# Eight early chunks in place of four in the output stage of a fused attention and spectral-mixing kernel

## The chip, the core and the metric

The kernel runs on one core of a Trainium2 chip. The metric is the device time of one execution in microseconds. The profile is of one execution; the timed runs are others. The engines are named as in the profile: PE is TensorE (PEld its weight loads), DVE is VectorE, ACT is ScalarE, POOL is GpSimd, SP is SyncE, which here only issues DMAs.

## What is computed

The first half is attention with a feature map, for 8 batches, 8 heads, 576 tokens and 64 features a head; the second half takes its output as x (8 batches, 576 tokens, 512 channels), mixes the 64 lowest frequencies of each sequence, and adds a rectified product.

```python
def _moe_ref(x, w_r, w_i, w_ch):
    X = np.fft.rfft(x, axis=1)
    Y = np.zeros_like(X)
    Xr, Xi = (np.real(X[:, :n_modes]), np.imag(X[:, :n_modes]))
    Yr = np.einsum('bmd,mde->bme', Xr, w_r) - np.einsum('bmd,mde->bme', Xi, w_i)
    Yi = np.einsum('bmd,mde->bme', Xr, w_i) + np.einsum('bmd,mde->bme', Xi, w_r)
    Y[:, :n_modes] = Yr + 1j * Yi
    y = np.fft.irfft(Y, n=S, axis=1)
    u = x + y
    return u + np.maximum(u @ w_ch, 0.0)
```

The weights w_r and w_i are 64 x 512 x 512 each in float32; most of what the kernel reads is these. The output is 8 x 576 x 512 float32, 9.44 MB.

## The kernel before

The core holds x in SBUF as `xs`, cut into 36 chunks `(bp, n)`: bp is one of four pairs of batches, n from 0 to 8; chunks 0 to 3 belong to the first batch of the pair, 4 to 7 to the second, and chunk 8 has rows of both. Every chunk has 128 tokens and 512 channels. A chunk's output is p + relu(q), where p = x + y and q = (x + y) w_ch. The kernel works with linearity: `xw` holds x w_ch of each chunk, and the contribution of the frequencies is added to both by matmuls with an inverse-transform table, from `yall` (the mixed frequencies) into p, and from `zall` (these times w_ch) into q.

The 64 frequencies are worked on in eight octets, `o` = 0 to 7. The weights of an octet come by GpSimd's DMA queue, in the order `wq`, into buffers of the pool `pw` (eight of them, tag "wt", which later also hold `yall`, `yl` and the output tiles). `mix` multiplies them; at the end of an octet its result is staged in `yst`, multiplied by w_ch into `zst`, and `put` copies both by DMA to their places: octets 0 to 6 to `yall` and `zall`, octets 6 and 7 also to `yl`, four copies at four groups of 32 partitions.

While the weights of the last groups arrive, `fill` takes pieces of other work from the list `todo`. A piece is the transposing of a chunk and its product with w_ch (`Channels`, 36 pieces, which also step through `inverse_tables`, where VectorE makes the tables CI, CD, CL and CM), or the adding of the octets that are already there (`Absorb`): octets 0 to 5 (96 rows of `yall` and `zall`) for most chunks, octets 0 to 6 (112 rows) for the early ones, which `full` puts last.

After the last octet stands the output stage, written out by hand as a list `seq` of `Last` objects: two single chunks, pairs of chunks, and two single chunks at the end. Each is one of these kinds:

- early: its last octet is added with table CM straight from `yst` and `zst` (`straight`), in full matmuls with 128 rows. These are chunks (0,0) to (0,3) before. The tiles hold eight batches' rows, so the table has zeros for all batches but the chunk's own.
- normal: octets 6 and 7 are added from `yl` with table CL (`late`), in matmuls with 32 rows that sit at different partitions for p and q and for the two chunks of the pair. x is brought into p by a matmul with the permutation `perm` (`base(0)`), xw into q by another (`base(1)`).
- later, "GpSimd pairs" below: chunks in `stored`, and the ninth chunks. Their x was written back to SBUF in the permuted order while filling (`back_x`), p gets no x on TensorE, and GpSimd adds x to the rectified q in SBUF (`relu`).

For all, ACT rectifies q out of PSUM into `rl` or `rx`, VectorE adds p and this into the output tile `of` (`ofr` for single chunks), and SP issues the store. Chunk (0,0) differs: ACT copies p into `rl` ahead of time (`keep_p`), and VectorE does max(q, 0) + rl in one instruction. q has four PSUM banks in turn (`bank`), p two double banks (`banks`), `rl` two buffers. All engines keep the program's order; `ahead` says which pair's q is worked on in front of which pair's p.

Of the kernel before, what the change touches and what calls it, by code (L numbers as in the profile page):

```python
# [43 lines left out]
def kernel(  # L44
# [536 lines left out]
    stored = [(1, 0), (1, 1), (1, 4), (1, 5), (2, 0), (2, 1), (2, 6), (2, 7), (3, 4), (3, 5)]  # L581
# [3 lines left out]
    CM = CF.rearrange("p c t x m -> p (c t x m)")[:, 0:512].rearrange("p (c s) -> p c s", c=4)  # L585


    def inverse_tables():
# [33 lines left out]
        jm, tm, rm, b0 = bits(pi, 5, 3), bits(pi, 4, 1), bits(pi, 3, 1), bits(pi, 0, 7)  # L622
        last = calc(calc(tm, 4.0, jm), 1.0, 56.0)
        b0 = calc(b0, 0.0, 1.0, ALU.is_equal, ALU.mult)
        yield
        for dst, m, r, only in ((CI, mode, r, None), (CL, late, r, None), (CM, last, rm, b0)):
            n = 512 if only is not None else 640
            ph = calc(r, -S_ / 4.0, S_ / 4.0)
            amp = calc(r, -4.0 / S_, 2.0 / S_)
            if m is mode:  # L630
                half = calc(calc(m, 0.0, -0.5, ALU.is_equal, ALU.mult), 1.0, 1.0)
                amp = calc(amp, half, 0.0)
            if only is not None:
                amp = calc(amp, only, 0.0)
            dve.tensor_scalar(out=ang[:, :n], in0=tok[:, :n], scalar1=m, scalar2=ph,
                              op0=ALU.mult, op1=ALU.add)
            dve.tensor_scalar(out=rnd[:, :n], in0=ang[:, :n], scalar1=1.0 / S_, scalar2=MAGIC,
                              op0=ALU.mult, op1=ALU.add)
            dve.tensor_scalar(out=rnd[:, :n], in0=rnd[:, :n], scalar1=-MAGIC,
                              scalar2=-float(S_), op0=ALU.add, op1=ALU.mult)  # L640
            dve.tensor_tensor(out=ang[:, :n], in0=ang[:, :n], in1=rnd[:, :n], op=ALU.add)
            yield
            act.activation(rnd[:, :n], ang[:, :n], ACT.Sin, scale=2.0 * math.pi / S_)
            if dst is CI:
                dve.tensor_scalar_mul(out=dst.rearrange("p c s -> p (c s)"), in0=rnd[:, :n],
                                      scalar1=amp)
                yield
                for a in range(2):
                    dve.tensor_copy(
                        CD.rearrange("k c (p a) -> k a c p", a=2)[:, a],  # L650
                        CI[:, 0:4].rearrange("k c (a p) -> k a c p", a=2)[:, a])
                yield
                continue
            for c in range(4):
                dve.tensor_scalar_mul(
                    out=dst[:, c, :].rearrange("k (p a) -> k a p", a=2),
                    in0=rnd[:, 128 * c:128 * c + 128].rearrange("k (a p) -> k a p", a=2),
                    scalar1=amp)
            if dst is CL:
                dve.tensor_scalar_mul(out=dst[:, 4, :], in0=rnd[:, 512:640], scalar1=amp)  # L660
            yield
# [46 lines left out]
    class Absorb:  # L708

        def __init__(self, bp, n):  # L710
            self.bp, self.n = bp, n
            self.table = CD if (bp, n) in stored else CI
            self.early = bp == 0 and n < 4
            self.rows = slice(0, 112 if self.early else 96)
# [71 lines left out]
    def put(src, o, dst, copies):  # L786
        if o < 7:
            sp.dma_start(dst[16 * o:16 * o + 16], src)
        if o > 5:
            for s in copies:  # L790
                r = 32 * s + 16 * (o - 6)
                (pool if o == 6 else act if s == 3 else sp).dma_start(yl[r:r + 16], src)


    class Last:

        def __init__(self, *items):
            self.items = items
            bp, n = items[0]
            self.early = bp == 0 and n < 4  # L800
# [32 lines left out]
        def straight(self, which):  # L833
            if self.early:
                for a, (bp, n) in enumerate(self.items):
                    pe.matmul((self.q if which else self.p)[a], lhsT=CM[:, n],
# [18 lines left out]
        def store(self):  # L855
# [5 lines left out]
            if n == 0 and self.first:  # L861
# [18 lines left out]
    seq = [Last((0, 0)), Last((0, 1))] + [Last(*x) for x in pairs[0][1:] + pairs[1] + pairs[2]]  # L880
    seq += [Last(*x) for x in pairs[3][:3]] + [Last((3, 6)), Last((3, 7))]
    seq.insert(11, Last((0, 8), (1, 8)))
    seq.insert(15, Last((2, 8), (3, 8)))
    H = DMODEL // 2
    while mixq:
# [4 lines left out]
        if not mixq:  # L890
            assert not todo
            seq[0].base(1)
            seq[0].late(1)
            seq[0].base(0)
            seq[0].late(0)
# [4 lines left out]
        if g == NG - 1 and i == 1:  # L900
            end = left == 0
            if end:
                seq[1].base(1)
                seq[1].late(1)
# [37 lines left out]
        else:  # L942
            fill(n)
    assert not todo
    seq[1].late(0)
    seq[2].base(1)
    seq[0].straight(1)
    seq[1].straight(0)
    seq[1].straight(1)
    seq[1].relu()  # L950
    ahead = {1: [2], 2: [3], 3: [4, 5], 4: [7], 5: [6], 6: [9], 7: [8], 8: [11], 9: [10], 10: [13],
             11: [12], 12: [15], 13: [14], 14: [17], 15: [16], 16: [18], 17: [19], 18: []}
    for g, s in enumerate(seq):
        ts = [seq[i] for i in ahead.get(g, [])]
        if ts and g not in (1, 3):
            ts[0].base(1)
        if g > 1 and g != 3:
            s.base(0)
        if g == 2:
            s.straight(0)  # L960
            seq[4].base(1)
            seq[3].base(0)
        for t in ts[:1]:
            t.late(1)
        if g > 2:
            s.late(0)
        for t in ts[:1]:
            t.straight(1)
            t.relu()
        s.store()  # L970
        for t in ts[1:]:
            t.base(1)
            t.late(1)
            t.relu()
# [31 lines left out]
```

## Time and profile before

| | |
|---|---|
| time, median of 4 runs (lowest to highest) | 443.27 us (442.14 to 444.83) |
| the profiled execution: time; span from first to last instruction | 441.98 us; 440.1 us |
| mean granted TensorE clock over the span | 0.909 |
| busy: PE, DVE, ACT, POOL | 334.7, 287.4, 282.7, 101.3 us |
| DMA read from and written to HBM | 163.64 MB, 9.44 MB |
| last weight lands | 403.52 us from the span's start |
| first and last store issued | 408.40 and 434.45 us |

A row of the table of stretches gives, for each stretch of time, its length, then the busy time of each engine with the number of its instructions, the granted clock, the mean busy share of the 16 DMA engines, and GB/s. The share can exceed 1 where packets overlap. A row of the timeline gives start, duration, engine, line, operation, the tile written and those read, with shapes; in square brackets stands how long the engine was idle before, and what it waited for. All rows carry line L37, the helper that issues every instruction, so tiles tell them apart: `pp` is p, `pt` is q, `of` the output of a pair.

### The profile page before, as it was taken

Reading aid. Unit: us, or ns where it says so; the run is one execution under the profiler, and the core shown is the slowest. Engines: PE = TensorE matmul, PEld = TensorE weight load, DVE = VectorE, ACT = ScalarE, POOL = GpSimd, SP = SyncE. Lnnn points to the kernel's source line nnn. Section 1 sums busy time; section 2 is a strip of 40 time slices with the busy share of each in tenths; the row PEclk is TensorE's granted clock in tenths of the full one; section 3 lists DMA queues with packets and bytes.
Section 4 is the critical chain, followed back from the end, with each engine's and each line's share of the span. In section 5 each row is a group of like instructions: output and inputs, shape, how many; then the busy total and the mean of one; then the engine's idle time right before and its main releaser. Section 6 shows DMA issues by size and latency. Waiting matters only on the chain.

```text
span 440.1 us, 10584 instructions
## 1 busy us (share of the span) xinstructions
PE 334.7 (76%) x4451; PEld 213.5 (49%) x4451; DVE 287.4 (65%) x563; ACT 282.7 (64%) x498; POOL 101.3 (23%) x142
## 2 busy tenths in 40 slices
PE   3567668777696677786886786947689999999992
PEld 2346547545565555664664564633345544433220
DVE  4667586555666766876777668638863343876694
ACT  4598687666878875985886768513544442665781
POOL 7132132121312212322322111131001120010391
PEclk9689888688989988997997899797999999999997
DMA  8999999999999999999999999999999999996697
GB/s 173 236 210 210 238 212 237 235 214 264 210 213 236 238 236 228 221 237 211 239 212 237 225 224 239 212 212 212 212 218 219 219 224 221 212 219 138 211 390 294
DMA packets 51584, 99.58 MB, mean 226 GB/s; under 512 B 2512, under 2 KB 13648, under 8 KB 51536
## 3 DMA queue, kind: packets, MB, share of 16 engines
q0 software_dynamic: 45376, 86.45, 99.7%
q1 hardware_dynamic: 6016, 12.32, 7.9%
q8 instruction: 35, 0.57, 0.5%
q10 hardware_dynamic: 144, 0.13, 0.2%
q14 instruction: 13, 0.11, 0.1%
HBM read 163.64 MB, written 9.44 MB: 393 GB/s over the span
## 4 chain that ended last, share of the span: by engine, by line
DMA 42%; issue 23%; PE 16%; DVE 7%; POOL 6%; ACT 4%; POOLq 0%; DVEq 0%; ACTq 0%
DMA wt<-in_moe_w_i_dram 29%; PE pt L37 12%; DMA vn<-in_v_dram 6%; DMA wt<-in_moe_w_r_dram 5%; POOL wt L37 3%; PE two L37 2%; PE one L37 1%; ACT AB L37 1%; ACT xw L37 1%; DVE xw L37 1%; POOL qb L37 1%; DMA out_dram<-of 1%; PE pp L37 1%; POOL kb L37 1%; DMA yl<-zst 1%
## 5 line engine op out<-in xcount | busy, mean ns | idle before, releaser
L37 ACT ACTIVATE AB<-two 128x1024 bf16<-128x1024 f32 x64 | 62.2, 1032 | 11.9 <-DVE mk L37 9.4
L37 ACT ACTIVATE AQ<-two 128x1024 bf16<-128x1024 f32 x64 | 62.9, 1051 | 3.6 <-PE two L37 3.4
L37 ACT CAST xw<-pt 128x512 bf16<-128x512 f32 x50 | 29.4, 587 | 40.7 <-PE pt L37 40.7
L37 DVE TENSOR_REDUCE mk<-two 128x8 f32<-128x1024 f32 x32 | 38.9, 1218 | 15.3 <-PE two L37 15.3
L37 DVE TENSOR_REDUCE m<-two 128x8 f32<-128x1024 f32 x32 | 39.2, 1224 | 12.9 <-PE two L37 12.7
L37 DVE RECIPROCAL rd<-one 128x6 f32<-128x6 f32 x48 | 9.4, 196 | 50.4 <-PE one L37 50.3
L37 DVE TENSOR_TENSOR va<-vn,ee 128x1152 bf16<-128x1152 f32 x32 | 42.0, 1355 | 0.0
L37 PE MATMUL pt<-wchb,xT 128*128 128x512 bf16 x136 | 35.8, 386 | 7.0 <-DVE xT L37 5.7
L37 POOL DMA_DIRECT2D wt<-in_moe_w_r_dram x30 | 22.3, 744 | 71.6 <-PE one L37 31.1
L37 POOL DMA_DIRECT2D wt<-in_moe_w_i_dram x28 | 20.9, 747 | 74.7 <-PE one L37 42.6
L37 PEld LDWEIGHTS <-xs 128*128 128x128 bf16 x624 | 31.6, 103 | 12.6 <-issue 7.7
L37 ACT COPY kT<-one 128x512 bf16<-128x512 bf16 (+1 forms) x32 | 19.2, 640 | 28.6 <-PE one L37 28.4
L37 PEld LDWEIGHTS <-minus 96*128 96x128 bf16 x288 | 27.7, 115 | 18.5 <-issue 13.4
L37 PE MATMUL two<-w2blk,qT 128*128 128x256 bf16 x128 | 20.3, 283 | 20.9 <-ACT AB L37 11.1
L37 PE MATMUL one<-wt,XT 128*32 128x512 bf16 x304 | 27.8, 452 | 9.8 <-DMA wt<-in_moe_w_i_dram 4.3
L37 PE MATMUL two<-qT,w2blk 128*128 128x512 bf16 x64 | 29.9, 467 | 4.4 <-ACT AQ L37 4.2
L37 PEld LDWEIGHTS <-qT 128*128 128x128 bf16 x144 | 13.8, 98 | 37.3 <-issue 35.1
L37 PE MATMUL two<-mT,minus 96*128 96x128 bf16 x256 | 30.3, 252 | 0.0
L37 POOL DMA_DIRECT2D kb<-in_k_dram x16 | 11.5, 718 | 75.5 <-PE one L37 74.7
L37 PE MATMUL one<-kvz,AQ 128*128 128x65 bf16 x512 | 28.0, 211 | 0.0
L37 DVE TENSOR_TENSOR xs<-one,rd 128x384 bf16<-128x384 f32 x48 | 26.8, 557 | 1.6
L37 PEld LDWEIGHTS <-XT 128*32 128x32 bf16 x512 | 14.4, 149 | 25.6 <-issue 12.3
(141 smaller groups left out, 725.8 us busy)
## 6 DMA issues: line engine op xcount, KB each, us to landing
wt<-in_moe_w_r_dram POOLq DMA_DIRECT2D x30, 1024.0 KB, 24.9
wt<-in_moe_w_i_dram POOLq DMA_DIRECT2D x28, 1024.0 KB, 24.7
vn<-in_v_dram POOLq DMA_DIRECT2D x15, 576.0 KB, 19.5
out_dram<-of SPq DMA_DIRECT2D x16, 512.0 KB, 3.4
kb<-in_k_dram POOLq DMA_DIRECT2D x16, 288.0 KB, 17.4
qb<-in_q_dram POOLq DMA_DIRECT2D x16, 288.0 KB, 17.2
xs<-in_moe_w_i_dram POOLq DMA_DIRECT2D x2, 1024.0 KB, 24.7
yacc<-in_moe_w_r_dram POOLq DMA_DIRECT2D x1, 1024.0 KB, 9.1
```

Of the source, the lines that this page charges most:

```text
L37: ins = f(*args, **kwargs)
```

## The change

The early chunks become (0,0) to (0,7). For the second batch of the first pair of batches a second table CM is made, whose zeros are elsewhere; CL and each CM are now written by one VectorE instruction over four chunks instead of four. The chunks (1,0), (1,1), (1,4), (1,5), (3,4) and (3,5) leave `stored`, (2,4) and (2,5) join it, so that there are three GpSimd pairs in place of five, besides the two pairs of ninth chunks. Chunk (0,1) is handled as (0,0) was. The last copy of `zst` into `yl`, which ACT's queue issued, is issued by SP. The order of the output stage is written anew: the pairs (1,0) to (1,6) are normal and follow each other, and the q of pair (2,0) is worked on behind pair (1,0).

```diff
--- before.py
+++ after.py
@@ -578,11 +578,12 @@
     CI = pb.tile([128, 5, 128], BF16, name="CI", bufs=1)
     CL = pb.tile([128, 5, 128], BF16, name="CL", bufs=1)
     CD = pb.tile([128, 4, 128], BF16, name="CD", bufs=1)
-    stored = [(1, 0), (1, 1), (1, 4), (1, 5), (2, 0), (2, 1), (2, 6), (2, 7), (3, 4), (3, 5)]
+    stored = [(2, 0), (2, 1), (2, 4), (2, 5), (2, 6), (2, 7)]
     perm = CF.rearrange("p c t x m -> p (c t x m)")[:, 512:640]
     dve.tensor_copy(perm.rearrange("k (p a) -> k a p", a=2),
                     ident_b.rearrange("k (a p) -> k a p", a=2))
-    CM = CF.rearrange("p c t x m -> p (c t x m)")[:, 0:512].rearrange("p (c s) -> p c s", c=4)
+    CM = [CF.rearrange("p c t x m -> p (c t x m)")[:, 0:512].rearrange("p (c s) -> p c s", c=4),
+          pb.tile([128, 4, 128], BF16, name="CM", bufs=1)]
 
 
     def inverse_tables():
@@ -619,19 +620,17 @@
         jt = calc(t, 4.0, j)
         mode = calc(bits(pi, 4, 7), 8.0, jt)
         late = calc(calc(bits(pi, 4, 1), 8.0, 48.0), 1.0, jt)
-        jm, tm, rm, b0 = bits(pi, 5, 3), bits(pi, 4, 1), bits(pi, 3, 1), bits(pi, 0, 7)
+        jm, tm, rm, b = bits(pi, 5, 3), bits(pi, 4, 1), bits(pi, 3, 1), bits(pi, 0, 7)
         last = calc(calc(tm, 4.0, jm), 1.0, 56.0)
-        b0 = calc(b0, 0.0, 1.0, ALU.is_equal, ALU.mult)
+        only = [calc(b, float(i), 1.0, ALU.is_equal, ALU.mult) for i in range(2)]
         yield
-        for dst, m, r, only in ((CI, mode, r, None), (CL, late, r, None), (CM, last, rm, b0)):
-            n = 512 if only is not None else 640
+        for dst, m, r in ((CI, mode, r), (CL, late, r), (CM, last, rm)):
+            n = 512 if dst is CM else 640
             ph = calc(r, -S_ / 4.0, S_ / 4.0)
             amp = calc(r, -4.0 / S_, 2.0 / S_)
             if m is mode:
                 half = calc(calc(m, 0.0, -0.5, ALU.is_equal, ALU.mult), 1.0, 1.0)
                 amp = calc(amp, half, 0.0)
-            if only is not None:
-                amp = calc(amp, only, 0.0)
             dve.tensor_scalar(out=ang[:, :n], in0=tok[:, :n], scalar1=m, scalar2=ph,
                               op0=ALU.mult, op1=ALU.add)
             dve.tensor_scalar(out=rnd[:, :n], in0=ang[:, :n], scalar1=1.0 / S_, scalar2=MAGIC,
@@ -651,11 +650,12 @@
                         CI[:, 0:4].rearrange("k c (a p) -> k a c p", a=2)[:, a])
                 yield
                 continue
-            for c in range(4):
+            for i in range(2 if dst is CM else 1):
                 dve.tensor_scalar_mul(
-                    out=dst[:, c, :].rearrange("k (p a) -> k a p", a=2),
-                    in0=rnd[:, 128 * c:128 * c + 128].rearrange("k (a p) -> k a p", a=2),
-                    scalar1=amp)
+                    out=(dst[i] if dst is CM else dst[:, 0:4]).rearrange(
+                        "k c (p a) -> k a c p", a=2),
+                    in0=rnd[:, 0:512].rearrange("k (c a p) -> k a c p", c=4, a=2),
+                    scalar1=calc(amp, only[i], 0.0) if dst is CM else amp)
             if dst is CL:
                 dve.tensor_scalar_mul(out=dst[:, 4, :], in0=rnd[:, 512:640], scalar1=amp)
             yield
@@ -710,7 +710,7 @@
         def __init__(self, bp, n):
             self.bp, self.n = bp, n
             self.table = CD if (bp, n) in stored else CI
-            self.early = bp == 0 and n < 4
+            self.early = bp == 0 and n < 8
             self.rows = slice(0, 112 if self.early else 96)
 
         def sum_p(self, p):
@@ -789,7 +789,7 @@
         if o > 5:
             for s in copies:
                 r = 32 * s + 16 * (o - 6)
-                (pool if o == 6 else act if s == 3 else sp).dma_start(yl[r:r + 16], src)
+                (pool if o == 6 else sp).dma_start(yl[r:r + 16], src)
 
 
     class Last:
@@ -797,7 +797,7 @@
         def __init__(self, *items):
             self.items = items
             bp, n = items[0]
-            self.early = bp == 0 and n < 4
+            self.early = bp == 0 and n < 8
             self.first = bp == 0 and n < 2
             self.later = n == 8 or items[0] in stored
 
@@ -833,7 +833,7 @@
         def straight(self, which):
             if self.early:
                 for a, (bp, n) in enumerate(self.items):
-                    pe.matmul((self.q if which else self.p)[a], lhsT=CM[:, n],
+                    pe.matmul((self.q if which else self.p)[a], lhsT=CM[n // 4][:, n % 4],
                               rhs=(yst, zst)[which], start=False, stop=True)
 
         def keep_p(self):
@@ -858,7 +858,7 @@
                 o = pw.tile([128, DMODEL], F32, name="ofr", tag="wt")
             else:
                 o = pw.tile([128, 2, DMODEL], F32, name="of", tag="wt")
-            if n == 0 and self.first:
+            if self.first:
                 dve.scalar_tensor_tensor(out=o, in0=self.q[0], scalar=0.0, in1=self.rl[:, 0],
                                          op0=ALU.max, op1=ALU.add)
             elif w == 1:
@@ -877,10 +877,9 @@
                 o.rearrange("p a e -> p (a e)") if w > 1 else o)
 
     pairs = [[((bp, n), (bp, n + 1)) for n in (0, 2, 4, 6)] for bp in range(NP)]
-    seq = [Last((0, 0)), Last((0, 1))] + [Last(*x) for x in pairs[0][1:] + pairs[1] + pairs[2]]
-    seq += [Last(*x) for x in pairs[3][:3]] + [Last((3, 6)), Last((3, 7))]
-    seq.insert(11, Last((0, 8), (1, 8)))
-    seq.insert(15, Last((2, 8), (3, 8)))
+    seq = [Last((0, 0)), Last((0, 1))] + [Last(*x) for x in pairs[0][1:] + pairs[1] + pairs[2][:3]]
+    seq += [Last(*pairs[3][0]), Last((0, 8), (1, 8)), Last(*pairs[3][1]), Last((2, 8), (3, 8))]
+    seq += [Last(*x) for x in (pairs[3][2], pairs[2][3])] + [Last((3, 6)), Last((3, 7))]
     H = DMODEL // 2
     while mixq:
         key = mixq.pop(0)
@@ -890,9 +889,7 @@
         if not mixq:
             assert not todo
             seq[0].base(1)
-            seq[0].late(1)
             seq[0].base(0)
-            seq[0].late(0)
         mix(*key, wts.pop(key), XTb[g % 2], bank)
         next_w(1)
         left = len(mixq)
@@ -901,7 +898,6 @@
             end = left == 0
             if end:
                 seq[1].base(1)
-                seq[1].late(1)
             py = pys.pop(o)
             yst = pb.tile([128, DMODEL], BF16, name="yst")
             pt = [bank([128, 2, 128], BF16) for h in range(2)]
@@ -942,36 +938,32 @@
         else:
             fill(n)
     assert not todo
-    seq[1].late(0)
+    seq[1].straight(0)
+    seq[1].keep_p()
     seq[2].base(1)
-    seq[0].straight(1)
-    seq[1].straight(0)
-    seq[1].straight(1)
-    seq[1].relu()
-    ahead = {1: [2], 2: [3], 3: [4, 5], 4: [7], 5: [6], 6: [9], 7: [8], 8: [11], 9: [10], 10: [13],
-             11: [12], 12: [15], 13: [14], 14: [17], 15: [16], 16: [18], 17: [19], 18: []}
-    for g, s in enumerate(seq):
-        ts = [seq[i] for i in ahead.get(g, [])]
-        if ts and g not in (1, 3):
-            ts[0].base(1)
-        if g > 1 and g != 3:
-            s.base(0)
-        if g == 2:
-            s.straight(0)
-            seq[4].base(1)
-            seq[3].base(0)
-        for t in ts[:1]:
+    for i in range(3):
+        seq[i].straight(1)
+    seq[2].relu()
+    seq[0].store()
+    seq[1].store()
+    ahead = [3, 4, 5, 6, 7, 8, 11, 10, 13, 12, 15, 14, 17, 16, 18, 19]
+    for g in range(2, len(seq)):
+        s, ts = seq[g], [seq[i] for i in ahead[g - 2:g - 1]]
+        for t in ts:
+            t.base(1)
+            t.straight(1)
+        s.base(0)
+        s.straight(0)
+        for t in ts:
             t.late(1)
-        if g > 2:
-            s.late(0)
-        for t in ts[:1]:
-            t.straight(1)
+        s.late(0)
+        for t in ts:
             t.relu()
         s.store()
-        for t in ts[1:]:
-            t.base(1)
-            t.late(1)
-            t.relu()
+        if g == 5:
+            seq[9].base(1)
+            seq[9].late(1)
+            seq[9].relu()
     pb_cm.__exit__(None, None, None)
     pw_cm.__exit__(None, None, None)
 
```

## The prediction

> **What bounds the kernel now.** I read four views: the table of stretches (who is busy when), the chain of waits, then the timeline of the tail for VectorE and TensorE. The tail is the only place where this change can move the end, and the first two views say why.
>
> ```profile
> core 0: us, PE busy (x) PEld busy (x) DVE busy (x) ACT busy (x) POOL busy (x), PEclk, DMA share, GB/s
> 380.00:385.00 5.00, 4.24 (x30) 1.97 (x29) 3.98 (x8) 3.42 (x7) 0.54 (x1) 1.00 1.12 212
> 390.00:395.00 5.00, 5.00 (x36) 1.82 (x28) 3.81 (x7) 3.17 (x7) 0.00 (x0) 1.00 1.12 219
> ...
> 403.50:408.00 4.50, 4.04 (x29) 2.02 (x29) 1.79 (x5) 1.54 (x4) 0.00 (x0) 1.00 0.28 68
> 408.00:412.00 4.00, 3.60 (x20) 1.23 (x19) 2.29 (x3) 2.33 (x5) 0.00 (x0) 1.00 0.84 197
> 412.00:416.00 4.00, 3.85 (x21) 0.99 (x21) 2.45 (x2) 3.77 (x8) 1.95 (x2) 1.00 0.60 245
> 416.00:420.00 4.00, 3.80 (x24) 1.07 (x23) 3.49 (x3) 3.04 (x7) 4.00 (x5) 1.00 0.68 274
> 420.00:424.00 4.00, 4.00 (x27) 1.19 (x26) 3.88 (x4) 3.56 (x8) 4.00 (x4) 1.00 1.01 407
> ...
> 432.00:436.00 4.00, 0.69 (x2) 0.09 (x1) 1.92 (x3) 0.00 (x0) 0.00 (x0) 0.88 1.02 398
> ```
>
> Up to 400 us the DMA engines are full with weights, and the chain of waits has one piece that says the same: the last weight lands at 403.52. After it come the last octet, then the stores. From 420 us the DMA engines are full again, with the output, at about 400 GB/s. Between 408 and 420 they are not: shares 0.84, 0.60, 0.68.
>
> ```profile
> 367.25 36.27 DMA wt<-in_moe_w_i_dram
> ...
> 407.27 4.11 DMA yl<-zst
> 411.42 0.39 PE pt L37 x2
> ```
>
> ```profile
> 409.90 1.22 DVE L37 TENSOR_TENSOR of<-pp,rl 128x1024 f32<-128x1024 f32 x1 [0.46 <-PE pp L37]
> 412.48 1.22 DVE L37 TENSOR_TENSOR of<-pp,rl 128x1024 f32<-128x1024 f32 x1 [1.36 <-ACT rl L37]
> 414.77 1.22 DVE L37 TENSOR_TENSOR of<-pp,rl 128x1024 f32<-128x1024 f32 x1 [1.07 <-PE pp L37]
> 416.35 1.22 DVE L37 TENSOR_TENSOR of<-pp,rx 128x1024 f32<-128x1024 f32 x1 [0.36 <-POOL rx L37]
> 417.50 1.21 DVE L37 TENSOR_TENSOR of<-pp,rl 128x1024 f32<-128x1024 f32 x1
> ```
>
> Each of these adds makes a pair of chunks ready for its store. A store of a pair is 524,288 bytes, 1.31 us at 400 GB/s; the adds come 2.6, 2.3 and 1.6 us apart, so the DMA engines starve. The cause is seen above: the fourth pair's sums need yl, which lands 4.11 us after its issue. TensorE itself stands still for little of this:
>
> ```profile
> 409.21 0.59 PE L37 MATMUL pp<-yst,CF 128*128 128x512 bf16 x2
> 411.42 0.39 PE L37 MATMUL pt<-yl,CL 32*128 32x512 bf16 x2 [0.41 <-DMA yl<-zst]
> 414.21 0.39 PE L37 MATMUL pt<-yl,CL 32*128 32x512 bf16 x2
> 414.22 0.39 PE L37 MATMUL pp<-yl,CL 32*128 32x512 bf16 x2
> 414.54 0.61 PE L37 MATMUL pt<-xw,CF 128*128 128x512 bf16 x2
> ```
>
> So the bound of the tail is three things in turn: the yl landing, TensorE's sums, the DMA engines.
>
> **The sums of the tail, part by part.** A full 128-row matmul follows the last one after 0.216 us (409.21, 409.42, ...). A pack of four 32-row matmuls starts at once (414.21 to 414.22), 0.31 after the full one before it, and the next full one starts 0.32 after the pack. So a normal pair (four full sums, four packed) takes about 3 x 0.216 + 0.31 + 0.32 = 1.28 us of TensorE, a GpSimd pair (no base sum of x) 0.216 + 0.31 + 0.32 = 0.85.
>
> *Pairs (0,4) and (0,6) become early.* They leave yl and take eight full matmuls: 8 x 0.216 = 1.73 us each instead of 1.28, together +0.9 us of TensorE. Here a rule speaks against the change. The Trainium skill (TensorEngine Tiling (Array Packing), Theoretical Speedup and Key Properties) gives four row tiles up to 4x and says that a change of mode drains the array. By it alone, the four last-octet sums of a pair cost one matmul, 0.216, against 0.86 straight: +0.65 a pair, +1.3 in all. The row has the drain in it (0.63 for switch, pack and return against 0.216 for no pack, so 0.41 for the pack) and gives +0.45 a pair. I take the row. It is paid for by removing the wait: the first use of yl moves from 410.6 to about 413.0.
>
> *Two GpSimd pairs fewer* (five to three beside the two pairs of ninth chunks). Four base sums more on TensorE, 4 x 0.216 = +0.86 us; four GpSimd adds of 1.15 us less, worth nothing, as VectorE waited 0.4 us in all for GpSimd. The 1.22 us of the VectorE adds is the same with GpSimd idle (409.90) and busy (417.50).
>
> *Second chunk like the first.* Its copy runs on ACT before zst is there, and VectorE takes the maximum in the same instruction (0.692 against 0.691 us). Its add starts at about 408.36 instead of 408.74. Bound: 0 to 0.4 us earlier for 256 KB.
>
> *The fourth yl copy goes from ACT's queue to SP's.* ACT loses 0.66 us of issue. SP issues it behind its twin at 407.81 to 408.36, just ahead of the first store (408.40 before): nothing, or 0.1 us. Landing: ACT's landed 4.11 us after issue, SP's 3.33; so 411.1 to 411.9, needed at 413.0. A cover of 1 us; if gone, pair (1,0) waits for the excess.
>
> *Tables and staging, 297 to 350 us.* Four chunks fewer are written back permuted: 16 transposes, four ACT copies of 0.59 us, and four VectorE copies at 0.42 instead of 0.72. CL is one write for four of 0.21 (one of 512 elements ran 0.54), CM two for four; two small instructions of 0.15 come in: between -1 and +1 us of VectorE, where a strided write may cost double. All lies under the weight stream (share 1.12), whose last transfer was issued 36 us before it landed. I count zero. If that cover were gone, TensorE would gain about 4 x 0.3 us. The eight early chunks are last in the filling work, the first at about 395; octet 6 landed at 390.1 and 392.4, so 3 us of cover. TensorE was done 0.6 us ahead of the last weight; the same number of pieces remains, so it stays.
>
> *The new order at the end*, worked forward with those rates, 0.10 us from matmul end to VectorE, 1.14 us from add to add, ACT 0.54 a bank, buffers released by the add two pairs earlier. The same rules give the rows of before to within 0.5 us (pair 17: 431.43, the trace 431.41). Starts of the adds of pairs 2 to 9:
> before 409.90, 412.48, 414.77, 416.35, 417.50, 418.63, 420.11, 421.25;
> after 410.1, 411.9, 413.2, 414.7, 417.1, 418.4, 419.6, 420.8.
> Pairs 3 to 5 gain 0.6 to 1.6 us. Then a new hole opens: at (1,0) the sums of (2,0)'s second half are inserted (0.85 us of TensorE), and the next pair's banks wait 0.2 us for ACT. So pair 6 gains 0.4, later pairs 0.2 to 0.5; the last add starts at 432.95 instead of 433.48.
>
> *The DMA engines* see first bytes 1.3 us after an issue, 1.31 us a pair, 0.36 to the landing; this gives the landings of pairs 2 to 11 before (414.1 to 428.6) within 0.2. Before, they never starve again from pair 5 on (pair 6 starts at 420.22). After, they starve about 1 us ahead of pair 6, which starts at 419.63; from there 12 pairs and two single chunks (17.0 us) are back to back, pairs 10 and 12 arriving just in time. Gain 0.59 us.
>
> *One thing in the store stream.* At 428.22 a 16 KB instruction packet holds one of the 16 DMA engines for 0.94 us; that engine's last store packets end at 438.4, the others' by about 437.3. The Trainium skill (Runtime: NRT & Kernel Launch, Instruction fetch mechanics) counts a block boundary as "mostly hidden", a price of 0; the row says 1.1 us at this end. The change takes 32 instructions off TensorE ahead of the tail (16 transposes with weight loads) and adds 8, so the fetch comes about 1 us later, still under the stores: 0 by either. I keep 1.1 us as a gain should it fall behind them, and 0.3 as a loss.
>
> Sum: 0.6 us less. The profiled execution took 441.98 (span 440.1 and 1.9 around it), so 441.4; it lies 1.3 under the median 443.27 of four, whose prediction is 442.7.
>
> **Rivals.**
> *The hole closes (gain 1.7 to 3.3).* Idle shares between 410 and 419 sum to 3.3 us. If pairs 2 to 6 came at the pace of DMA, all of it would go: 440.0. The schedule of TensorE speaks against it. A milder form is the instruction fetch falling behind the stores: 0.6 + 1.1 = 1.7, 441.6. Chance together 0.22.
> *TensorE becomes the bound, slower.* Place: pairs 5 to 8, four normal pairs in a row, where before normal and GpSimd pairs alternated (2.63 us for two). If each costs 0.3 more than my 1.28, as the first such pairs of before did (412.80 to 414.54, 1.74), the add of pair 8 starts 1.2 later, at 420.8; ten pairs and two singles then give an end 0.6 later than before: 443.9. It decides from 0.15 us a pair on. For it: +1.8 us of matmuls in a stretch where TensorE is at 3.85 of 4; against it: before's slow pair waited for banks that ACT held, which is rarer here. Chance 0.25.
> *It doesn't do what it says:* yl lands later behind its twin, or a slot of the store buffers is held, and pair 5 waits as pair 3 did. Then the gain is 0: 443.3. Chance 0.13. The main case has 0.40.
>
> **How the numbers follow.** About 0.5% (2.2 us) is what a measurement of this kernel can tell from no change. The likeliest case and most of each rival lie within it. Faster takes the upper half of the first rival, 0.14; slower the tail of the second and what I don't see in the filling work, 0.14; same 0.72. The range reaches from the first rival's middle, 440.7, to the second's 443.9 with half the spread of the runs (442.14 to 444.83) on it, 444.7.
>
> **What would show it.** Right: no wait for yl on TensorE; adds of pairs 3 to 5 at 411.9, 413.2, 414.7; a gap of about 2.3 us ahead of pair 6; DMA share 1.0 from 419.6; last weight still at 403.5. Wrong: a last mix later than 403.6, adds of pairs 6 to 8 more than 1.5 us apart, or VectorE waiting for a landing of a store before pair 15.

## The result: 0.27% faster, and the profile after

The changed kernel takes 441.71 us (median of 37 runs, 440.73 to 443.56), the kernel before 442.85 us (56 runs, 441.83 to 445.32): a ratio of 0.9973, 95% interval 0.9965 to 0.9982, so 0.8 to 1.5 us less. The forecast was 442.7 against 443.27, 0.6 us less, within 0.5%. The profiled execution took 441.39 us (span 439.6).

The first view to read is the table of stretches of the tail:

```profile
core 0: us, PE busy (x) PEld busy (x) DVE busy (x) ACT busy (x) POOL busy (x), PEclk, DMA share, GB/s
403.50:408.00 4.50, 4.16 (x30) 2.06 (x29) 1.82 (x5) 2.65 (x6) 0.00 (x0) 1.00 0.28 69
408.00:412.00 4.00, 4.00 (x20) 1.76 (x18) 2.51 (x3) 2.22 (x5) 0.00 (x0) 1.00 0.65 191
412.00:416.00 4.00, 4.00 (x22) 1.31 (x21) 3.19 (x3) 2.92 (x6) 0.00 (x0) 1.00 0.67 273
416.00:420.00 4.00, 4.00 (x25) 1.22 (x24) 2.88 (x3) 3.34 (x8) 2.27 (x2) 1.00 0.65 267
420.00:424.00 4.00, 4.00 (x24) 1.04 (x24) 3.66 (x5) 3.60 (x7) 3.23 (x3) 1.00 0.99 404
```

TensorE is now busy without a break from 408 to 424 (4.00 of 4.00), where before it stood still for a little in three stretches. The DMA engines are no better fed: 0.65, 0.67, 0.65, against 0.84, 0.60, 0.68. The starving was not removed; what was a wait for yl is now TensorE's own pace.

The timeline of TensorE and that of VectorE show the two steps of the schedule, pair 5's first use of yl and the hole ahead of pair 6:

```profile
412.86 0.59 PE L37 MATMUL pp<-yst,CM 128*128 128x512 bf16 x2
413.39 0.39 PE L37 MATMUL pt<-yl,CL 32*128 32x512 bf16 x2
...
415.01 0.61 PE L37 MATMUL pt<-xw,ident_b 128*128 128x512 bf16 x2
415.54 0.39 PE L37 MATMUL pt<-yl,CL 32*128 32x512 bf16 x2
415.86 0.75 PE L37 MATMUL pt<-xw,CF 128*128 128x512 bf16 x2
```

```profile
410.53 1.22 DVE L37 TENSOR_TENSOR of<-pp,rl 128x1024 f32<-128x1024 f32 x1 [1.22 <-ACT rl L37]
412.25 2.52 DVE L37 TENSOR_TENSOR of<-pp,rl 128x1024 f32<-128x1024 f32 x2 [0.50 <-PE pp L37]
415.26 1.23 DVE L37 TENSOR_TENSOR of<-pp,rl 128x1024 f32<-128x1024 f32 x1 [0.48 <-DMA out_dram<-of]
417.53 3.82 DVE L37 TENSOR_TENSOR of<-pp,rl 128x1024 f32<-128x1024 f32 x3 [1.05 <-PE pp L37]
```

No bracket stands behind the yl matmul at 413.39: the wait is gone (the last copy landed at 411.91). The bracket of pair 5's add at 415.26 names the landing of a store, one of the signs of being wrong; but TensorE's p for it had ended only at 415.18, and in the runs a_pad16 and a_thin16 below the same wait (0.48 and 0.49 us) is put down to TensorE, so no buffer was held there. Pairs 2 to 5 are added at 410.53, 412.25, 413.55 (the second of the x2) and 415.26, and 2.27 us pass before pair 6, while TensorE works on the second half of (2,0) (ident_b, 415.01) and the banks free up (0.75 instead of 0.60 at 415.86).

Two executions are best compared from one event on, the landing of the last weight, which was at 403.52 before and 403.86 after. In these times, add starts and ends:

| us behind the last weight | before | after |
|---|---|---|
| adds of pairs 2, 3, 4, 5 | 6.38, 8.96, 11.25, 12.83 | 6.67, 8.39, 9.69, 11.40 |
| adds of pairs 6, 8, 12 | 13.98, 16.59, 21.71 | 13.67, 16.27, 21.52 |
| add of pair 16 | 26.40 | 26.40 |
| last add | 29.96 | 29.59 |
| end of span | 36.56 | 35.75 |

The pairs' lead has gone by pair 16; the last add gains 0.37 us and the end 0.81. So what was gained stands behind the add of pair 16, in the last stores. The DMA view of the stretch from 424 to 437 us, before and then after, shows it (queues: packets, MB, share of the 16 engines; then the stores, with the median time from issue to landing):

```profile
q1 hardware_dynamic: 1767, 5.10, 99.7%
q8 instruction: 1, 0.02, 0.5%
q14 instruction: 1, 0.01, 0.1%
...
out_dram<-of SPq DMA_DIRECT2D x8, 512.0 KB, 4.9
```

```profile
q1 hardware_dynamic: 1768, 5.10, 99.8%
q14 instruction: 1, 0.01, 0.1%
...
out_dram<-of SPq DMA_DIRECT2D x8, 512.0 KB, 3.2
```

Before, a 16 KB instruction packet (queue 8) stands among the stores, and they take 4.9 us to land; after, there is none of queue 8, and they take 3.2. After the change the packet that came at 428.22 comes at 440.18, behind the last store. The last DMA engine then ends 0.5 us behind the bulk of the others (437.8 and 437.3), where it was 1.1 us before (438.4 and 437.3). A smaller packet, 8 KB of queue 14, stands at about 436 us in both, and in every run below near the end of the stores.

The late landings reach VectorE too, because a pair's add needs a free output buffer. The add of pair 17, before and then after:

```profile
431.41 1.23 DVE L37 TENSOR_TENSOR of<-pp,rx 128x1024 f32<-128x1024 f32 x1 [0.27 <-DMA out_dram<-of]
```

```profile
431.40 1.21 DVE L37 TENSOR_TENSOR of<-pp,rx 128x1024 f32<-128x1024 f32 x1
```

Before, it waited for the store issued at 426.48, which landed at 431.29; after, no landing holds it.

### The profile page after: what moved, and what is told of

Same layout as the page of the kernel before. It is cut to its first block, busy times and chain, and to the rows that moved or that the text cites. A ratio compares the mean times of both kernels' runs of the same rounds, so it can differ in the third digit from the quotient of the medians.

```text
span 439.6 us, 10549 instructions
## 1 busy us (share of the span) xinstructions
PE 339.7 (77%) x4439; PEld 216.7 (49%) x4439; DVE 285.9 (65%) x560; ACT 281.0 (64%) x494; POOL 96.9 (22%) x138
## 4 chain that ended last, share of the span: by engine, by line
PE 23%; DMA 22%; issue 22%; ACT 15%; DVE 13%; POOL 4%; POOLq 0%; ACTq 0%; DVEq 0%
DMA wt<-in_moe_w_i_dram 14%; PE one L37 10%; PE two L37 7%; DMA wt<-in_moe_w_r_dram 7%; ACT AB L37 6%; DVE mk L37 4%; DVE m L37 4%; PE pt L37 4%; ACT AQ L37 3%; POOL wt L37 2%; PE pp L37 2%; ACT XT L37 2%; DMA vn<-in_v_dram 2%; DVE XT L37 2%; ACT kT L37 1%
## 5 line engine op out<-in xcount | busy, mean ns | idle before, releaser
L37 PEld LDWEIGHTS <-xs 128*128 128x128 bf16 x624 | 31.3, 102 | 12.8 <-issue 7.5
L37 PE MATMUL two<-w2blk,qT 128*128 128x256 bf16 x128 | 22.8, 308 | 18.6 <-ACT AB L37 8.7
L37 PEld LDWEIGHTS <-qT 128*128 128x128 bf16 x144 | 14.8, 105 | 35.9 <-issue 32.6
L37 POOL DMA_DIRECT2D kb<-in_k_dram x16 | 11.5, 718 | 84.1 <-PE one L37 83.3
L37 PE MATMUL two<-w2blk,kT 128*128 128x256 bf16 x128 | 21.0, 292 | 7.6 <-ACT AB L37 7.6
```

Of the source, the lines that this page charges most:

```text
L37: ins = f(*args, **kwargs)
```

## The experiments

All are timed against the kernel before, 11 to 22 runs each. "First add" and "end" are of the profiled execution, behind the last weight; "packet" is the start of the 16 KB packet in the stretch of the stores; "lag" is the last DMA engine's end behind the bulk of the others; "16 to end" is the time from the start of the add of pair 16 to the end of the span.

| run | ratio (95%) | first add | end | packet | lag | 16 to end |
|---|---|---|---|---|---|---|
| before | 1 | 4.16 | 36.56 | 428.2 | 1.1 | 10.16 |
| after | 0.9973 (0.9965 to 0.9982) | 4.16 | 35.75 | none | 0.5 | 9.35 |
| a_pad16 | 0.9991 (0.9981 to 1.0001) | 4.15 | 36.40 | 428.6 | 1.1 | 10.00 |
| a_thin16 | 0.9976 (0.9960 to 0.9993) | 4.47 | 36.68 | 428.0 | 1.1 | 9.96 |
| a_pad64 | 1.0011 (0.9998 to 1.0025) | 5.90 | 38.25 | 423.8 | 0.6 | 9.37 |
| b_pad64 | 1.0079 (1.0053 to 1.0106) | 6.47 | 38.82 | 420.4 | 0.6 | 9.57 |
| b_thin60 | 0.9986 (0.9972 to 1.0001) | 4.51 | 37.28 | 420.0 | 0.6 | 9.45 |
| b_less54 | 1.0008 (0.9990 to 1.0026) | 5.48 | 37.51 | 418.7 | 0.6 | 9.71 |
| a_early4 | 1.0036 (1.0022 to 1.0051) | 4.42 | 38.82 | none | 0.6 | 9.35 |
| a_early4b | 0.9988 (0.9972 to 1.0003) | 4.75 | 37.67 | 431.8 | 1.1 | 9.97 |
| b_early8 | 0.9986 (0.9967 to 1.0005) | 4.18 | 36.69 | 427.7 | 1.1 | 10.70 |
| a_hole6 | 0.9975 (0.9962 to 0.9987) | 4.16 | 35.95 | none | 0.6 | 9.36 |
| a_one | 0.9975 (0.9962 to 0.9988) | 4.16 | 35.66 | none | 0.6 | 9.34 |
| a_actput | 0.9989 (0.9972 to 1.0006) | 4.16 | 36.79 | none | 0.6 | 9.37 |

### The instruction packet

Can the packet's place be the other half of the gain? The trace before has 35 packets of queue 8 for 8902 matmuls and weight loads of TensorE, one for about 254, so its place can be moved by instructions that do nothing. In the changed kernel, 16 transposes of k were done twice:

```diff
+    again = []
...
                     pe.transpose(ptr[:, j - lo, :], rows[:, j * 128:(j + 1) * 128], ident_b)
+                    if flat and len(again) < 16 and units.index(self) > 5:
+                        again.append(pe.transpose(ptr[:, j - lo, :],
+                                                  rows[:, j * 128:(j + 1) * 128], ident_b))
```

> The changed kernel with 16 transposes of k done twice in the attention phase (32 instructions more on TensorE, same values), so that TensorE's stream is as long ahead of the tail as before the change. Theory A (part of the gain is the instruction packet that left the store stream): a 16 KB packet of queue 8 falls between 425 and 433 again, one DMA engine ends 1.0 us after the others instead of 0.5, and the time from the last weight's landing to the end of the span is 0.5 us longer than the 35.75 us of the changed kernel: ratio to before about 0.9985. Theory B (the gain is all from the earlier sums): no difference from the changed kernel, 0.9973.

The same DMA view of this run, 424 to 437 us:

```profile
q1 hardware_dynamic: 1728, 5.09, 99.5%
q8 instruction: 1, 0.02, 0.6%
...
out_dram<-of SPq DMA_DIRECT2D x8, 512.0 KB, 4.8
```

The packet is back, at 428.6, and the stores take 4.8 us again. First add and all adds up to pair 16 are where the changed kernel has them, to 0.02 us (26.40 for pair 16 in both); the end is 0.65 us later. The ratio moves from 0.9973 to 0.9991, 0.8 us, with intervals that just overlap. Theory A (the packet's place matters) holds here.

The second run puts the same 32 instructions elsewhere, as other work:

```diff
                 ps = one([128, 2, 128])
+                for _ in range(2 if 1 <= units.index(self) <= 4 else 0):
+                    pe.matmul(ps[:, 0, 0:1], lhsT=tT[:, 8, :], rhs=w2blk[:, 0:1],
+                              start=True, stop=True)
```

> The changed kernel with 16 one-column matmuls (32 instructions with weight loads, overwritten by the next matmul) early in the attention phase: the same 32 instructions as in the run with 16 transposes, but of other work at another place. Theory A (the packet's place decides): first add 4.2 us behind the last weight, adds as in the changed kernel, a 16 KB packet at about 428 to 429, last DMA engine 1.0 to 1.1 us behind the others, end 0.5 to 0.7 us later than the changed kernel's: ratio 0.9985 to 0.999. Rival (the loss with 16 transposes was TensorE time in the attention phase): 0.9973.

The packet came at 428.0 and the lag was 1.1 us, as expected. The first add was 0.31 us later than in the changed kernel, so of its 0.93 us at the end 0.62 are the packet's. The time, 0.9976 with an interval of 0.9960 to 0.9993, can't tell it from the changed kernel. In the times, then, the packet's cost is seen once and once not.

The profiles settle it, because the tail from the add of pair 16 on is the same work in all kernels with the new order (last column of the table). In the six without a 16 KB packet there it took 9.34 to 9.37 us (after, a_hole6, a_one, a_actput, a_early4, and a_pad64, whose packet came 11 us earlier); in the three with one, a_pad16, a_thin16 and a_early4b, 9.96 to 10.00. That is 0.6 us, with nothing between the two groups, whatever was edited ahead.

From the other side, the packet was to be taken out of the stores of the kernel before. Three ways were tried, the first with 64 transposes, and with a control on the changed kernel:

> The kernel before with 64 transposes of k done twice in the attention phase (128 instructions more on TensorE, same values), so that the packet of 428.22 moves about 12 us earlier, to about 416, where the DMA engines have idle time. Theory A: the last store lands 0.6 to 1.0 us earlier, 36.56 us from the last weight to the end become 35.6 to 36.0: ratio 0.998. Theory B: nothing, 1.000. If the 64 transposes cost time in the attention phase, the last weight lands later than 403.5.

> The changed kernel with 64 transposes of k done twice in the attention phase: a control for what such instructions cost. Theory A: its last packet falls at about 416 to 420, in the idle time of the DMA engines, so it ends as the changed kernel does, ratio 0.9973, with the last weight at the same place within the spread. If repeated transposes cost time by themselves, it is slower than the one with 16.

Both missed. Each is slower, by 0.8% and, against the changed kernel, 0.4%: the first add comes 6.5 and 5.9 us behind the last weight instead of 4.2. So 64 transposes in the attention phase delay the filling work until it, and no longer the last weight, starts the tail. Their times say nothing of the packet; the lag is 0.6 us in both. But their profiles show what the packet did where it fell, in the row of VectorE that b_pad64 has for pair 8:

```profile
423.77 1.23 DVE L37 TENSOR_TENSOR of<-pp,rl 128x1024 f32<-128x1024 f32 x1 [0.71 <-DMA out_dram<-of]
```

The add waited for the landing of a store, as that of pair 17 did in the kernel before. So moving the packet forward does not make it free: it can hold an add in the middle instead of the end.

> The kernel before with 60 one-column matmuls (120 instructions with their weight loads, overwritten by the next matmul) in the second to sixth unit of the attention phase, where TensorE has slack, so that the packet of 428.22 falls at about 417 to 418, where the DMA engines still have idle time, and the first add stays 4.2 us behind the last weight. Theory A (a 16 KB packet among the saturated stores costs the end 0.5 to 0.8 us): packet ends of the last DMA engine 0.5 us after the others instead of 1.0, end of span 0.5 us earlier from the last weight, ratio 0.998 to 0.999. Theory B (the packet is harmless): 1.000. If the first add is later than 4.2 us behind the last weight, the filling work was pushed again and the times tell nothing; then only the packet ends do.

With the one-column matmuls of a_thin16, six a call in units 1 to 5, the push is only 0.35 us, and the lag is 0.6. But the packet fell at 420.0, not at 417 to 418, and made itself felt in another way. In the timeline of VectorE:

```profile
422.03 1.22 DVE L37 TENSOR_TENSOR of<-pp,rx 128x1024 f32<-128x1024 f32 x1
424.37 1.23 DVE L37 TENSOR_TENSOR of<-pp,rl 128x1024 f32<-128x1024 f32 x1 [1.12 <-PE pp L37]
```

TensorE's sums for that add had ended at 423.1, so the wait was not for them, though the bracket names TensorE. A store landed at 424.25, just ahead of the add; with the row of b_pad64 above, a held output buffer is the likely cause. The ratio, 0.9986, includes 1, and counted from the first add the end is 0.37 us later than in the kernel before (32.77 against 32.40), so this run shows no gain.

```diff
                     for c in range(5):
+                        if c == 3 and units.index(self) < 9:
+                            continue
```

> The kernel before without 54 of the 480 matmuls of the forward transform (the fourth of five partial sums in the first nine units is left out, so the frequencies miss a share), 108 instructions less on TensorE, nothing changed in the tail. The packet of 404.5 then falls at about 412, where the DMA engines starve, and that of 428.2 behind the last store. Theory A (about half of the gain of the change is that packet): adds as before from the last weight (last one 29.8 to 30.0 behind it), last DMA engine 0.5 us behind the others instead of 1.0, end 0.5 to 0.6 us earlier from the last weight, ratio 0.9987. Theory B (the packet is harmless): 1.000. The work left out can shorten the attention phase too, but the last weight is set by the DMA stream and should stay at 403.5 within its spread.

Fewer instructions did not give an earlier tail either: the first add came 5.48 us behind the last weight, 1.3 late. The packet did not leave as planned but fell at 418.7. Counted from the first add, the end is at 32.03 us, against 32.40 in the kernel before: 0.37 us less with the same order of work, and the last of the stores landed thus:

```profile
q1 hardware_dynamic: 1681, 5.18, 101.1%
...
out_dram<-of SPq DMA_DIRECT2D x9, 512.0 KB, 3.7
```

The expectation of the time failed (1.0008); that of the lag held. Together: with the new order the packet among the last stores costs 0.6 us (nine profiles), in the kernel before about 0.4 (one run, corrected for its late start).

### The early chunks

```diff
-            self.early = bp == 0 and n < 8
+            self.early = bp == 0 and n < 4
```

(in both classes; all else as changed)

> The changed kernel with only chunks (0,0) to (0,3) early, all else (order, fewer GpSimd pairs, second chunk) as changed. My schedule: the sums of pair 3 wait for yl, its add starts at 413.4 instead of 412.25, pair 6 at 418.3 instead of 417.5, and the last add 1.1 us later; the end 1.2 us after the changed kernel's, so about as before or 0.1% slower: ratio 0.9995 to 1.001. Rival (the early extension costs TensorE what it saves in waiting, and the new order brings the gain): same as the changed kernel, 0.997.

Both theories missed: it is 0.63% slower than the changed kernel, and in the profiled execution the last add comes 32.67 us behind the last weight, 3.1 later. The timeline of TensorE and the table of stretches say why:

```profile
409.05 0.59 PE L37 MATMUL pp<-yst,CF 128*128 128x512 bf16 x2
411.31 0.73 PE L37 MATMUL pt<-yl,CL 32*128 32x512 bf16 x2 [1.67 <-DMA yl<-zst]
...
413.27 0.97 PE L37 MATMUL pt<-xw,CF 128*128 128x512 bf16 x2
414.04 1.06 PE L37 MATMUL pp<-xs,CF 128*128 128x512 bf16 x2
```

```profile
411.00:413.00 2.00, 1.69 (x10) 0.55 (x10) 0.00 (x0) 1.09 (x2) 0.00 (x0) 1.00 0.75 298
413.00:415.00 2.00, 2.00 (x9) 0.46 (x8) 1.22 (x1) 1.09 (x2) 0.00 (x0) 0.59 0.25 100
415.00:417.00 2.00, 2.00 (x9) 0.53 (x8) 1.20 (x1) 1.08 (x2) 0.00 (x0) 0.55 0.51 213
```

TensorE stands still for 1.67 us, and from 413.37 to 416.79 it has half its clock (column PEclk, 0.59 and 0.55 over these stretches): two matmuls take 1.06 us instead of 0.59. To see whether a shorter standstill keeps the clock, the base sums of pairs 3 and 4 were put ahead of the wait, as the kernel before had them (on top of the edit above):

```diff
         for t in ts:
-            t.base(1)
+            if g != 3:
+                t.base(1)
             t.straight(1)
-        s.base(0)
+        if g != 3:
+            s.base(0)
         s.straight(0)
+        if g == 2:
+            seq[4].base(1)
+            seq[3].base(0)
```

> The changed kernel with four early chunks, and with the base sums of pairs 3 and 4 ahead of the first use of yl, as the kernel before had them, so that TensorE stands still for 0.8 us instead of 1.7 us. Theory C (in the run with four early chunks 1.9 us of the 3.1 us came from the halved TensorE clock between 413.4 and 416.8 that followed the standstill): granted clock 1.00 throughout, last add 0.9 to 1.1 us later than the changed kernel's from the last weight (30.6 instead of 29.6), ratio to before 0.999 to 1.001. Rival (the late yl alone costs 3 us): as with four early chunks and no covering, ratio 1.0036, last add 32.5 behind the last weight.

```profile
PE pt L37 <- DMA yl<-zst: 0.8, 1, 0.8
```

```profile
411.00:413.00 2.00, 1.11 (x8) 0.30 (x8) 0.62 (x1) 0.65 (x2) 0.00 (x0) 1.00 0.71 258
413.00:415.00 2.00, 1.89 (x11) 0.60 (x11) 1.45 (x2) 1.63 (x4) 0.00 (x0) 1.00 0.57 234
```

With 0.8 us of standstill the clock stays at 1.00, and the last add is at 30.89. From the first add it is 0.7 us later than in the changed kernel, against 2.8 in the run above. So the rival is out: of the 3.1 us, about 2 came from the longer standstill and the halved clock together. The two are not parted, and each run has one profile. What the four more early chunks bring, with the wait covered as well as before, is about 0.7 us of adds; the ratio, 0.9988, has the packet in it, which came at 431.8 here.

The reverse is the kernel before with the early chunks alone (the second table, n < 8, `straight(0)` for pairs 3 and 4; order and stored chunks as before):

> The kernel before with one part of the change alone: chunks (0,0) to (0,7) early with the second table, and the table's new instructions; the stored chunks, the order and the second chunk stay. Theory (the GpSimd pair (1,0) behind them has to come later for this to help): no wait for yl, adds of pairs 3 and 4 at 8.4 and 9.7 behind the last weight instead of 9.0 and 11.3, but pair 5 waits for its GpSimd adds and starts at about 12.8 as before, later pairs as before; packet at about 428 as before; ratio 1.000 within 0.001. Rival (the early chunks bring the gain by themselves): pair 5 at about 11.5, ratio 0.998.

```profile
411.93 1.22 DVE L37 TENSOR_TENSOR of<-pp,rl 128x1024 f32<-128x1024 f32 x1 [0.91 <-ACT rl L37]
414.27 1.23 DVE L37 TENSOR_TENSOR of<-pp,rl 128x1024 f32<-128x1024 f32 x1 [1.11 <-PE pp L37]
415.81 1.22 DVE L37 TENSOR_TENSOR of<-pp,rx 128x1024 f32<-128x1024 f32 x1 [0.32 <-POOL rx L37]
```

Pair 3 gains 0.4 us, pair 5 waits for GpSimd as expected and comes at 12.41 instead of 12.83, later pairs keep that 0.4, and pair 4 missed its 9.7 (10.87). The ratio of 0.9986, 0.9967 to 1.0005, settles nothing between the two theories, and the profile bears out neither: pair 5 stands between their 12.8 and 11.5, and pair 16 comes at 25.99, 0.4 us ahead of the kernel before and of the changed kernel (26.40 in both). The end is where it was (36.69) because the last adds and stores lost the lead again: the packet at 427.7 took 1.45 us here, a store issued at 425.96 landed only at 431.30, and pair 17's add started at 431.42, though its own p had ended at about 429.9.

Counted from the first add, pair 16 comes at 22.24 us in both kernels, at 21.80 with the early chunks alone (b_early8) and at 22.94 with the rest of the change and four early chunks (a_early4b). So the early chunks brought 0.4 to 0.7 us of adds, and the new order with fewer GpSimd pairs gave about as much back. Whether the early chunks in the old order would be faster with the packet elsewhere was not tried.

### The hole, the second chunk and the queue

```diff
-        if g == 5:
+        if g == 6:
             seq[9].base(1)
```

> The changed kernel with the second half of (2,0) worked on behind pair 6 instead of behind pair 5. Theory (TensorE sets the pace from 407 to 420, so the hole only moves): the add of pair 6 starts 1.1 us earlier (12.6 behind the last weight instead of 13.7), that of pair 7 at the same time as before the move (15.0), the end the same within 0.1 us, ratio 0.9973. Rival (the hole ahead of pair 6 starves the DMA engines and sets the end): the end 0.5 us earlier, ratio 0.996.

```profile
415.28 2.50 DVE L37 TENSOR_TENSOR of<-pp,rl 128x1024 f32<-128x1024 f32 x2 [0.48 <-PE pp L37]
419.03 2.52 DVE L37 TENSOR_TENSOR of<-pp,rl 128x1024 f32<-128x1024 f32 x2 [1.26 <-PE pp L37]
```

The hole moved: pair 6 came 1.0 us earlier (12.67, the second of the x2 at 415.28), pair 7 at 15.15, the end 0.2 us later, the ratio the same. TensorE sets the pace up to about 420 us, and moving this hole one pair on changed the end by no more than 0.2 us.

```diff
-    seq[1].keep_p()
...
+    seq[1].relu()
     seq[2].relu()
...
-            if self.first:
+            if n == 0 and self.first:
```

> The changed kernel with the second chunk as it was: ACT rectifies q behind the straight sums and VectorE adds p. Theory (this part is worth nothing at the end, since the stores starve later): the add of the second chunk starts 0.3 to 0.5 us later, ACT's work on pair 2 shifts by 0.5 us, pair 2's add by 0.2 to 0.5, pair 3's and later ones not; end the same within 0.1 us, ratio 0.9973. Rival (it frees ACT and the banks in the starving stretch): 0.3 us slower, 0.998.

The second chunk's add came 0.24 us later (5.00), pair 2's a little earlier (6.59), the end was the same (35.66; 0.9975). This part is worth nothing by itself; the shift of pair 2 was expected with the wrong sign.

```diff
-                (pool if o == 6 else sp).dma_start(yl[r:r + 16], src)
+                (pool if o == 6 else act if s == 3 else sp).dma_start(yl[r:r + 16], src)
```

> The changed kernel with the last yl copy issued by ACT again. Theory: first store issued 0.3 to 0.6 us earlier, that copy lands between 411.4 and 412, ahead of its use at 13.0 us - 3.5 us = 9.5 us behind the last weight; later adds and the end within 0.1 us; ratio 0.9973. Rival (SP's queue held the first stores back): end 0.3 us earlier, 0.9965; or ACT's 0.66 us of issue delays its copy for the second chunk and pair 2 by 0.5 us, with the same end.

Here the expectation missed. All adds from pair 2 on come 1.0 us later and the end 1.04 us (0.7 us by the medians' ratios, 0.9989, with intervals that overlap). ACT's timeline, then TensorE's:

```profile
407.43 0.63 ACTq L37 DMA_DIRECT2D yl<-zst  x1
408.10 0.58 ACT L37 COPY rl<-pp 128x512 f32<-128x512 f32 x1 [1.08 <-PE pp L37]
```

```profile
407.41 0.39 PE L37 MATMUL pp<-zst,CF 128*128 128x512 bf16 x1
408.74 0.38 PE L37 MATMUL pp<-zst,CF 128*128 128x512 bf16 x1 [0.94 <-ACT rl L37]
```

ACT has to wait for zst before it can issue the copy, and the copy of p of the second chunk stands behind that issue. TensorE's next sum goes into the q of the same double bank and waits for this copy. In the changed kernel the copy runs at 407.26, under the wait for zst. In the kernel before, the next work of ACT behind its issue at 407.27 had to wait for TensorE in any case (408.11, 1.24 us of idle time), so nothing was lost. So the two edits belong together: the second chunk's early copy needs the issue to leave ACT's queue.

## Why the forecast was right, and where it was off

*What bounds the tail.* Held: first the yl landing, then TensorE, then the DMA engines. The schedule was close. Shifted by the 0.34 us of the later last weight, the adds of pairs 2 to 9 came at 410.2, 411.9, 413.2, 414.9, 417.2, 418.5, 419.8, 420.9, within 0.2 us of the working, the last at 433.1 against 432.95. The hole of 2.3 us ahead of pair 6 was there, and pairs 7 and 8 followed after 1.30 us each, against 1.28 worked out, so the rival of a slower TensorE is out. One sign of being wrong did appear, a last weight later than 403.6; but in five other profiles of the new order it landed between 403.23 and 405.10, so the 0.34 us is within the spread.

*The rule on array tiling.* The row served better than the rule. Pairs 3 and 4 follow after 1.72 and 1.30 us, which is eight and six full matmuls of 0.216. In the timeline after the change two full matmuls, a pack and the return still take 0.85 us (415.01 to 415.86), the 0.216 + 0.31 + 0.32 of the working; with a pack at the price of one matmul it would be 0.65.

*The store stream, 0.59.* Mis-sized. With the packet in both, the end counted from the first add goes from 32.40 to 32.24 and 32.21 (a_pad16, a_thin16): 0.2 us. With the packet outside the last stretch in both (b_less54, after), from 32.03 to 31.59: 0.4 us. The schedule's own share is 0.2 to 0.4, and it shows only in the stores: pair 16, which was to gain 0.2 to 0.5, gained nothing.

*The instruction packet, 0.* The step that failed: I let the fetch come 1 us later, still under the stores, and kept the other case as a gain of 1.1. It fell behind them, and that brought 0.4 to 0.6 us. So the forecast came near in part by luck: a schedule taken at 0.59, where it brought 0.2 to 0.4, and a packet taken at nothing added up to 0.6, where the profiles differ by 0.8. The Trainium skill (Runtime: NRT & Kernel Launch, Instruction fetch mechanics) calls the crossing of a block boundary mostly hidden; in this tail it costs about 0.14% (0.6 of 442 us), by the runs that brought it back. By TensorE's instructions I counted 24 fewer, which is right (8902 and 8878 matmuls and weight loads in the profiles). At 428.22 the kernel before had about 30 left to its last matmul, so 24 fewer would have put the fetch at about 431 to 432, still among the stores; in a_early4b it came there, at 431.81, in the changed kernel behind the end. What decides between the two the records do not show.

*The queue move, nothing or 0.1.* Wrong in its working: I asked how late yl would be, and not what stood behind ACT's issue. It hid in the sum because the second chunk's part was drawn up with the move in it.

*What is left.* The profiles differ by 0.81 us behind the last weight, the medians by 1.14. The profiled execution of before lay 0.9 us under its median, that of after 0.3, so this rest may be the draw. The lighter filling work (16 transposes fewer) may also keep the first add in its place in more executions: the runs with 64 more transposes had it 1.7 and 2.3 us late, but the one with less work (b_less54) had it 1.3 late too. That stays open. The forecast held 0.5% for what a measurement can tell from no change; with 56 and 37 runs the interval is 0.17% wide, so a change of 0.27% can be told from none.

## What to carry to other kernels

Where a tail is bound by one unit after another, removing the first wait uncovers the next; work the schedule forward to the last unit before counting the idle time as gain. Where a store stream saturates the DMA engines at the end, look for instruction packets of the long instruction stream inside it, and remember that a few instructions more or less far ahead move them, so that an unrelated edit may win or lose half a microsecond. To see an effect of this size, time a stretch of the profile that is the same work in all variants: here it repeated to 0.03 us in six profiles, where the times of 22 runs leave 0.1% (0.4 us) open on either side. Before an engine that issues a DMA is freed or loaded, list what waits behind the issue on its queue.

## What was not expected of the hardware

A standstill of TensorE of 1.67 us was followed by half the clock for 3.4 us, beginning 2 us after the standstill had ended (413.37 to 416.79), and the two together lost about 2 us; behind one of 0.8 us the clock stayed whole. This is one profile of each. The Trainium skill (TensorE: Matmul & The Clock Gate, Part 1: The HAM clock gate) gives free-running windows of about 3.4 us and an idle window as the cause; the length of the slow stretch agrees, but here TensorE had been idle for less than half of the 3.4 us ahead of it (about 1.35 us).

A 16 KB instruction packet (0.9 to 1.5 us long) in a saturated stream raised the median time to landing of the 512 KB stores in the last stretch from 3.2 to 4.8 us, more than its own length, and through the output buffers it reached VectorE's adds. It set the last DMA engine back by 0.6 us.
